# Starting the folded weight sums of the second layer earlier, in a four-batch attention and two-layer kernel

## The chip, the cores and the metric

The kernel runs on one core of a Trainium2 chip. The metric is the device time of one execution in microseconds (us). The engines are named as in the profile: PE (matmuls) with PEld (its weight loads), DVE (vector), ACT (scalar), POOL, and SP, which here only issues transfers (DMAs). POOL issues transfers too.

## The reference, cut to what matters

For 4 batches of 576 tokens, 8 heads and 32 memory slots: a softmax of `phi` over the sequence sums k and v into 32 slots per head, and the queries attend to these slots. The result, 2304 tokens by 512, goes through two layers:

```
x1 = square(relu(x @ moe_w_in)) @ moe_w_out          # 512 -> 2048 -> 512
h  = x1 @ moe2_w_in                                  # 512 -> 2048
out = (h * tanh(softplus(h))) @ moe2_w_out           # 2048 -> 512
```

## The kernel before, in words

Every float32 operand of a matmul is split into a high part (`float32r`) and a rest, and three products are summed.

**First layer.** `a_tile(b, half, f0, f1, ...)` takes 288 tokens (half of batch b) through the slices `fc` of 128 hidden units: six matmuls give `h`, ACT makes `s` from it (relu at L586, square at L587), then `g` and its rest are made (on DVE for the last batch, L593 and L594), and twelve matmuls (L540 to L542) add to four accumulators `a`, three slices later. For batches 0 and 1 the 16 slices are cut in groups of 4, 6 and 6, so there are 12 tiles, numbered `i` from 0 to 11 in the loop over `subs`. Then come the tiles (2,0), (2,1), (3,0) and (3,1), each with all 16 slices. One slice is called a step here.

**Second layer.** It is done with seven products in place of eight for each pair of 256-wide blocks (Strassen's scheme in Winograd's form). Its left operands are sums of blocks of x1 (`y_work`), its right operands sums of blocks of the weights. The weight sums are made ahead by the class `Fold`: of two raw units (512 KB each) it makes one pair, that is seven parts of 256 KB, and stores them in DRAM (`wf_i2`, `wf_o2`). There are 32 raw units (`raw_i2_0` to `15`, `raw_o2_0` to `15`; the profile leaves the 2 away), so 16 pairs. A part is cast by ACT into a stage buffer `st` (L299), DVE subtracts for the rest (L300), and POOL issues the store (L301). `Fold.tick` is called once a step: it starts a unit when it may (ACT L264), and takes one or two of the pending part steps of a pair. A stage buffer is free again when its store has landed.

**Where units are folded.** The first `EARLY` units use three raw buffers of the pool Y, which also holds the attention tiles. After tile (2,1) the loop `while fold.busy()` writes down the rest of those; the scheduler of the framework, which orders each engine's instructions by its own estimate of time, lets them run into tile (3,0). Then Y is closed and the remaining units use a pool CV in its place, ticked from tiles (3,0) and (3,1) (`tick3`).

**The seam.** After tile (3,1), `now` counts the units of the second layer: `h_step` multiplies one part `u` (loaded by `feed` from DRAM, eight ahead, L909) with a left operand, six matmuls `hb` of 384 columns (L964 to L966). ACT copies the first of a block's products out of PSUM into `ht` (L979). The parts `u57`, `u59`, ... of `wf_o2` have a second set of eight buffers, and their loads may be issued as soon as the parts are stored.

SP, ACT, DVE and POOL each work through their instructions in the order written for them, so a waiting instruction holds back all behind it on its engine.

The k and v of batch 2, first half (`kv20`, 1 MB), are loaded by `load_kv` into the one buffer with the tag "kv"; PE needs it for the sums `pk` of batch 2, in tile `i` = 10.

Of the kernel before, what the change touches and what calls it, by code (L numbers as in the profile page):

```python
# [8 lines left out]
F32R = mybir.dt.float32r  # L9
# [9 lines left out]
P = 128  # L19
# [8 lines left out]
LAG = 3  # L28
# [2 lines left out]
TT = 768  # L31
HT = TT // 2
ROLE = [0, 1, 2, 3, 0, 2, 3]
EARLY = 22


def body(tc, q, kvm, kvt, phi, w_in1, w_out1, w_in2, w_out2, out):
    nc = tc.nc

    def open_pool(name, side):  # L40
        cm = tc.tile_pool(name=name, bufs=1, side=side, reuse_waits="tile")
        return cm, cm.__enter__()
# [14 lines left out]
    cm_y, Y = open_pool("y", "right")  # L57
# [9 lines left out]
    at = (0, TAIL)  # L67
# [8 lines left out]
    def load_phi(b, p):  # L76
        nc.sync.dma_start(phi_t[p][:, at[p]:at[p] + S], phi[b, p])

    def load_kv(b, p):

        t = Y.tile([P, 2, 4, NC, D], F32, tag="kv", name=f"kv{b}{p}", bufs=1)
        nc.sync.dma_start(
            t.rearrange("p s g c d -> p s (g c d)"), kvm[b, p].rearrange("s p x -> p s x"))
        kv_t[b, p] = t

    def load_tail(b):
        t = Y.tile([P, 2, 4, D], F32, tag="kt", name=f"kt{b}", bufs=1)
        nc.sync.dma_start(
            t.rearrange("p s g d -> p s (g d)"), kvt[b].rearrange("s p x -> p s x"))
        kt_t[b] = t  # L90
# [47 lines left out]
    @contextlib.contextmanager  # L138
    def behind(table, key):

        if key is None:
            yield
        else:
            with tc.issue_after(table[key].ins):
                yield

    class Conv:
# [20 lines left out]
        def tick(self, start=True, between=None):  # L168


            ends = [x for x in self.flight if x[2] == 2]
            bits = [x for x in self.flight if x[2] == 1]
            for x in ends:
                key, u = x[0], x[1]
                if (key, u // 2) not in wt:
                    wt[key, u // 2] = tuple(
                        wo.tile([P, 2, DM], F32R, tag=f"wo{part}{u // 2}", name=f"{key}{part}{u // 2}")
                        for part in "hl")
                x[4] = [w[:, u % 2, :] for w in wt[key, u // 2]]
                nc.scalar.copy(x[4][0], x[3])  # L180
            if start and self.started < min(self.loaded, self.limit) and self.ready(*self.order[self.started]):
                key, u = self.order[self.started]
                high = self.raw[key, u][:, :, 1].bitcast(F32)
                with behind(marks, "step" if self.paced else None):
                    nc.scalar.activation(high, high, AF.Prelu, scale=2.0 ** -112, alpha=-2.0 ** 32)
                self.started += 1
                self.flight.append([key, u, 0, None, None])
            with behind(marks, self.after):
                self.fields(bits, ends, between)
            for x in self.flight:  # L190
                x[2] += 1
            for x in list(self.flight):
                if x[2] == 3 or (x[2] == 2 and x[0] == "i1"):
                    self.done.add((x[0], x[1]))
                    self.flight.remove(x)
# [38 lines left out]
    class Fold:  # L234
# [23 lines left out]
        def tick(self, start=True):  # L258
            todo, self.bits = self.bits, []
            if start and self.started < self.loaded and len(self.steps) < 5:  # L260
                key, u = self.order[self.started]
                high = self.raw[key, u][:, :, 1].bitcast(F32)
                with behind(marks, "step"):
                    nc.scalar.activation(high, high, AF.Prelu, scale=2.0 ** -112, alpha=-2.0 ** 32)  # L264
                self.started += 1
                self.bits.append((key, u))
            for key, u in todo:
                self.fields(key, u)
            for _ in range(2):
                if self.steps:  # L270
                    self.steps.pop(0)()

# [144 lines left out]
    def kv_unit(b, tag, nxt):  # L417
        for p in range(2):
            if b > 1:
                kv_soft(b, p)  # L420
                yield
            kv_turn(b, p)
            yield
            kv_mem(b, p, (0, 1), tag)
            nxt(p)
            yield
        kv_heads(b, (0, 1), tag)
        yield
# [97 lines left out]
    def drain(*lanes):  # L526
        while any(lanes):
            for lane in lanes:
                run_step(lane)
# [126 lines left out]
    def lazy(f):  # L656
        yield from f()

    def soft_both(b):
        kv_soft(b, 0)  # L660
        kv_soft(b, 1)
        yield

    def kv_later(b):
        def nxt(p):
            if p == 0 and b > 1:
                load_kv(b, 1)
            if b + 1 < B:
                load_phi(b + 1, p)
                if p == 1:  # L670
                    load_kv(b + 1, 0)
                    load_tail(b + 1)
        u = lazy(lambda: kv_unit(b, "b0", nxt))

        return [[u, 3], [iter(range(2)), 2], [u, 4]] if b > 1 else [[u, 5]]
# [17 lines left out]
    fold = Fold([(key, u) for key in ("i2", "o2") for u in range(NF)])  # L693
    fold.cap = EARLY

    def stage_0(n):
        if n % 2 == 0:
            return X.tile([P, 2, 256], F32R, tag="ys0", name=f"st{n}", bufs=2)
        return Y.tile([P, 2, 256], F32R, tag=("x", "at")[n // 2 % 2], name=f"st{n}", bufs=1)
# [4 lines left out]
    def stage_y(n):  # L704
        return Y.tile([P, 2, 256], F32R, tag=f"ys{2 + n // 2 % 2}", name=f"st{n}", bufs=2)

    fold.pool, fold.stage = Y, stage_0

    def load_page(j):

# [4 lines left out]
    for i, (f0, f1, b, half) in enumerate(subs):  # L715
        final = i == len(subs) - 1
        if i == 0:
            u = lazy(lambda: attn_unit(0, 1, lambda: load_q(1, 1)))
            lanes = [[u, 1], [soft_both(1), 1], [u, 3]] + kv_later(1) + attn_later(1, 0)
            n_steps = 3  # L720
        elif i == 1:
            assert (0, 1) in a_t
            c1.limit, c1.after, c1.paced = 2 * GROUPS[0] + 3, (0, 1), True
            n_steps = 1
        elif i == 2:
            drain(lanes)
            c1.limit, c1.after = len(c1.order), (1, 0)
            lanes, n_steps = [[iter(range(1)), 1]] + attn_later(1, 1), 1
        elif i == 3:
            drain(lanes)  # L730
            c1.after = (1, 1)
        elif i == 4:
            c1.after = None
        elif i == len(subs) - 2:
            lanes, n_steps = kv_later(2), 2
        elif final:
            drain(lanes)
            lanes, n_steps = attn_later(2, 0), 1
            load_page(0)
            load_page(1)  # L740

        def tick(fc):
            if len(c1.done) < 2 * NF:
                c1.tick()
            else:
                if not fold.loaded:
                    fold.load(3)
                if i == 10 and fc == f0 + LAG + 1:
                    fold.stage = stage_x
                if i > 9 or i == 9 and fc > f0:  # L750
                    fold.tick(start=fc % 2 == 0)

        def mid(fc):
            run_step(lanes, n_steps)

        def post(fc):
            if fc % 2 == half == 0 and fc + 2 < f1 and i != 2:
                c1.need("i1", fc + 3)
                w_part(b, fc // 2 + 1, 0, 256)
            if i == 1 and fc + 1 == f1:  # L760
                w_part(1, fc // 2, 0, 256)
            if i % 4 == 0:
                if fc >= f0 + 2:
                    c1.need("o1", fc - 2)
                if fc + 1 == f1:
                    c1.need("o1", fc)
            if half == 1 and fc + 2 == f1 and not final:

                if b == 0:
                    w_part(1, f0 // 2, 0, 256)  # L770
                else:
                    c1.need("i1", f1 + 1)
                    w_part(0, f1 // 2, 0, 256)
            if final and fc < f1 - 1:
                w_part(2, fc - f0, 0, 256)
                if fc < f1 - 2:
                    load_page(fc - f0 + 2)

        if i == 0:
            w_part(0, 0, P, 2 * P)  # L780

        a_tile(b, half, f0, f1, tick, mid, post, ("mm",) if i in (0, 1, 6) else ("mm", "b0"))
    drain(lanes)


    def tick2(fc):
        if fc == LAG + 1:
            fold.stage = stage_y
        fold.tick(start=fc % 2 == 0)

    b, nb = 2, 3
    lanes = [attn_later(b, 1), [[iter(range(2)), 2]] + kv_later(nb)]
# [283 lines left out]
    for now, (kind, i, one, two) in enumerate(plan):  # L1076
# [10 lines left out]
        if now + AHEAD < len(plan) and plan[now + AHEAD][0] == "b":  # L1087
            _, _, j, k = plan[now + AHEAD]
# [51 lines left out]
```

## Time and profile before

| what | value |
|---|---|
| median of 3 runs | 788.1 us (787.21 to 789.16) |
| the profiled execution, its own time | 790.56 us |
| its span, first to last instruction | 788.8 us |
| PE, PEld busy share of the span | 94%, 89% |
| DVE, ACT, POOL busy share | 67%, 54%, 17% |
| mean granted TensorE clock | 0.974 of full speed |

The shares are averages over stages that differ; a stage is read by its own stretch of time. Tiles 0 to 11 run to about 225 us, (2,0) and (2,1) to about 320 us, (3,0) and (3,1) to 412 us, and the second layer from there. Matmuls overlap, so the time of one is best read from start to start.

### The profile page before, as it was taken

To read this page: it belongs to the slowest core of one execution; us is meant where nothing else is said; L and a number is where in the kernel's file an instruction comes from. 1 tells how busy PE (TensorE), PEld (TensorE's weight loads), DVE (VectorE), ACT (ScalarE), POOL (GpSimd) and SP (SyncE) were. 2 spreads that over 40 slices of the span, in tenths; PEclk is the share of its full clock that TensorE was granted. 3 is DMA by queue.
4 is the path that set the end of the run, shared out by engine and by line. 5 is a ranking of instruction groups with operands and counts; after the bars stand their busy time and mean duration, and the time that the engine had idled before them with its cause. 6 is when DMAs were issued, how large, how long until landed. Compare 5 with 4: busy or idle time off the path is not lost.

```text
span 788.8 us, 16341 instructions
## 1 busy us (share of the span) xinstructions
PE 739.4 (94%) x5984; PEld 700.1 (89%) x5984; DVE 526.0 (67%) x1072; ACT 427.3 (54%) x960; POOL 136.3 (17%) x176
## 2 busy tenths in 40 slices
PE   5699999999899999989996799999999999999997
PEld 4488898998778888889995799899999999999997
DVE  3979846455757678768884559774558784556683
ACT  3577856565656677756654236452436552434552
POOL 0000000011111112232232414240112140111040
PEclk8699999999999999999998999999999999999999
DMA  9992535039888676786779978789788889788881
GB/s 333 406 406 72 187 100 195 28 124 299 279 294 297 214 246 220 258 341 208 290 254 343 295 247 292 240 268 301 240 262 251 247 265 303 244 258 251 247 265 62
DMA packets 89440, 195.85 MB, mean 248 GB/s; under 512 B 9872, under 2 KB 22672, under 8 KB 89360
## 3 DMA queue, kind: packets, MB, share of 16 engines
q1 hardware_dynamic: 80400, 165.45, 64.1%
q0 software_dynamic: 8960, 29.37, 9.6%
q8 instruction: 47, 0.77, 0.4%
q14 instruction: 33, 0.27, 0.1%
HBM read 151.78 MB, written 42.99 MB: 247 GB/s over the span
## 4 chain that ended last, share of the span: by engine, by line
PE 57%; issue 24%; POOL 7%; DMA 5%; DVE 3%; ACT 3%; SPq 1%; POOLq 0%; DVEq 0%; ACTq 0%
PE hb L964 7%; PE hb L965 7%; PE hb L966 7%; POOL wf_o L301 3%; POOL wf_i L301 3%; PE a L540 3%; PE a L541 3%; PE a L542 3%; DMA raw_i<-in_moe_w_in_dram 2%; PE h L578 1%; PE h L580 1%; PE h L579 1%; PE pw L478 1%; DMA wf_o<-st 1%; DMA u<-wf_i 1%
## 5 line engine op out<-in xcount | busy, mean ns | idle before, releaser
L540 PE MATMUL a<-g,o1h 128*128 128x288 f32 x512 | 150.5, 302 | 2.5 <-DVE ys L555 1.9
L541 PE MATMUL a<-g,o1l 128*128 128x288 f32 x512 | 149.0, 299 | 0.0
L542 PE MATMUL a<-g,o1h 128*128 128x288 f32 x512 | 132.5, 298 | 4.8 <-DVE g L594 4.8
L1009 DVE TENSOR_TENSOR opl<-a,oph 128x384 fp32r<-128x384 f32 x144 | 101.2, 723 | 50.8 <-ACT oph L1008 50.5
L964 PE MATMUL hb<-ych,u 128*128 128x384 f32 x336 | 114.8, 342 | 11.8 <-ACT ht L979 7.5
L965 PE MATMUL hb<-ycl,u 128*128 128x384 f32 x336 | 114.3, 340 | 0.0
L966 PE MATMUL hb<-ych,u 128*128 128x384 f32 x336 | 111.2, 340 | 0.0
L1008 ACT CAST oph<-a 128x384 fp32r<-128x384 f32 x144 | 73.5, 513 | 66.0 <-PE b20b L1030 5.9
L540 PEld LDWEIGHTS a<-g,o1h 128*128 128x128 f32 x512 | 97.2, 190 | 8.7 <-ACT s L586 2.9
L542 PEld LDWEIGHTS a<-g,o1h 128*128 128x128 f32 x512 | 90.3, 190 | 8.6 <-DVE g L594 6.3
L541 PEld LDWEIGHTS a<-g,o1l 128*128 128x128 f32 x512 | 97.5, 191 | 0.4 <-issue 0.4
L970 ACT ACTIVATE a<-hs 128x384 f32<-128x384 f32 x72 | 37.6, 525 | 92.2 <-DVE hs L974 92.2
L578 PE MATMUL h<-ah,wp 128*128 128x288 f32 x256 | 80.6, 316 | 5.8 <-ACT wp L484 2.8
L586 ACT ACTIVATE s<-h 128x288 f32<-128x288 f32 x128 | 52.2, 410 | 56.3 <-PE h L580 52.1
L301 POOL DMA_DIRECT2D wf_i<-st x56 | 30.3, 543 | 285.5 <-DVE st L300 278.6
L580 PE MATMUL h<-ah,wp 128*128 128x288 f32 x256 | 76.4, 299 | 0.7 <-DVE wp L485 0.7
L579 PE MATMUL h<-al,wp 128*128 128x288 f32 x256 | 76.7, 300 | 0.3 <-DVE al L468 0.3
L964 PEld LDWEIGHTS hb<-ych,u 128*128 128x128 f32 x336 | 64.3, 191 | 13.0 <-ACT ht L979 7.9
L594 DVE TENSOR_TENSOR g<-s,g 128x288 fp32r<-128x288 f32 x128 | 57.3, 450 | 26.4 <-ACT g L591 25.3
L974 DVE TENSOR_TENSOR hs<-hu,hb 128x384 f32<-128x384 f32 x72 | 39.5, 552 | 46.2 <-PE hb L966 45.8
L578 PEld LDWEIGHTS h<-ah,wp 128*128 128x128 f32 x256 | 48.7, 191 | 18.4 <-ACT s L586 5.3
L965 PEld LDWEIGHTS hb<-ycl,u 128*128 128x128 f32 x336 | 64.1, 191 | 0.0
(255 smaller groups left out, 1747.8 us busy)
## 6 DMA issues: line engine op xcount, KB each, us to landing
u<-wf_i SPq DMA_DIRECT2D x168, 256.0 KB, 3.7
u<-wf_o SPq DMA_DIRECT2D x168, 256.0 KB, 3.2
raw_i<-in_moe_w_in_dram SPq DMA_DIRECT2D x32, 512.0 KB, 5.1
raw_o<-in_moe_w_out_dram SPq DMA_DIRECT2D x32, 512.0 KB, 5.7
wf_i<-st POOLq DMA_DIRECT2D x56, 256.0 KB, 4.8
wf_o<-st POOLq DMA_DIRECT2D x56, 256.0 KB, 5.3
win1r<-w_i SPq DMA_DIRECT2D x17, 512.0 KB, 5.6
kv<-in_kvm_dram SPq DMA_DIRECT2D x5, 1024.0 KB, 9.0
```

The costliest lines, as they stand in the source:

```text
L301: nc.gpsimd.dma_start(wf[key][k, :, j], st.bitcast(F32).rearrange("p s o -> p (s o)"))
L540: nc.tensor.matmul(o, wh[:, c, cs], sh, start=first, stop=False)
L541: nc.tensor.matmul(o, wl[:, c, cs], sh, start=False, stop=False)
L542: nc.tensor.matmul(o, wh[:, c, cs], sl, start=False, stop=last)
L578: nc.tensor.matmul(ph, w[:, 0, hg, fs], hi[:, hg], start=(hg == 0), stop=False)
L579: nc.tensor.matmul(ph, w[:, 0, hg, fs], lo[:, hg], start=False, stop=False)
L580: nc.tensor.matmul(ph, w[:, 1, hg, fs], hi[:, hg], start=False, stop=(hg == 1))
L964: nc.tensor.matmul(ps, wh, yh[:, d], start=(j < 4 and d == 0), stop=False, **kw)
L965: nc.tensor.matmul(ps, wh, yl[:, d], start=False, stop=False, **kw)
L966: nc.tensor.matmul(ps, wl, yh[:, d], start=False, stop=end, **kw)
L1008: nc.scalar.copy(hi, x)
L1009: sub(lo, x, hi.bitcast(F32))
```

## The change

- `EARLY` goes from 22 to 26: four more units are folded in Y, four fewer in CV (six for ten).
- `Fold.tick` takes two part steps only while more than four are pending, otherwise one.
- The condition that let the fold tick only from the second step of `i` = 9 is gone: it ticks as soon as the first layer's weights are all converted.
- The first pair's parts use the "kv" buffer as four stage slots (`parts`), so `kv20` is no longer loaded at the end of batch 1's work but at the start of `i` = 9; new stage functions give the next parts other free tiles.
- In tiles (2,0) and (2,1) a unit may start at every third step, before at every second.

```diff
-EARLY = 22
+EARLY = 26
...
-            for _ in range(2):
+            for _ in range(2 if len(self.steps) > 4 else 1):
                 if self.steps:
                     self.steps.pop(0)()
...
                 if p == 1:
-                    load_kv(b + 1, 0)
+                    if b > 1:
+                        load_kv(b + 1, 0)
                     load_tail(b + 1)
...
+    def stage_k(n):
+        if not parts:
+            parts.append(Y.tile([P, 4, 2, 256], F32R, tag="kv", name="parts", bufs=1))
+        return parts[0][:, n % 4]
+
+    def stage_a(n):
+        return Y.tile([P, 2, 256], F32R, tag=("x", "at", "et")[n % 3], name=f"st{n}", bufs=1)
...
-    fold.pool, fold.stage = Y, stage_0
+    fold.pool, fold.stage = Y, stage_k
...
-                if i == 10 and fc == f0 + LAG + 1:
-                    fold.stage = stage_x
-                if i > 9 or i == 9 and fc > f0:
-                    fold.tick(start=fc % 2 == 0)
+                if i == 9 and fc == f0:
+                    fold.stage = stage_a
+                    load_kv(2, 0)
+                elif i in (9, 10) and fc == f0 + LAG + 1:
+                    fold.stage = stage_0 if i == 9 else stage_x
+                fold.tick(start=fc % 2 == 0)
...
     def tick2(fc):
         if fc == LAG + 1:
             fold.stage = stage_y
-        fold.tick(start=fc % 2 == 0)
+        fold.tick(start=fc % 3 == 0)
```

**At the seam, on ACT.** Before, from the last part of tile (3,1)'s accumulators on (`ys` is the copy of an accumulator, `ht` the first copy of the second layer):

```order
L299 CAST st_5335<-raw_o_15_5060 128x256
L557 COPY ys_5541<-a_4938 128x288
L299 CAST st_5193<-raw_o_13_4855 128x256
L557 COPY ys_5551<-a_4940 128x288
L299 CAST st_5227<-ct_o_12_5057 128x256
L299 CAST st_5373<-raw_o_15_5060 128x256
L299 CAST st_5331<-ct_o_14_5262 128x256
L299 CAST st_5461<-ct_o_14_5262 128x256
L299 CAST st_5368<-raw_o_15_5060 128x256
L299 CAST st_5424<-raw_o_15_5060 128x256
L299 CAST st_5428<-ct_o_14_5262 128x256
L979 COPY ht_5572<-hb_5565 128x384
```

Now, from the last cast of a part (all of the 16 pairs done) to the same copy:

```order
L299 CAST st_5126<-ct_o_14_4926 128x256
L586 ACTIVATE s_12_5386<-h_12_5377 128x288
L587 ACTIVATE s_12_5386<-s_12_5386 128x288
L586 ACTIVATE s_13_5432<-h_13_5423 128x288
L586 ACTIVATE s_14_5461<-h_14_5452 128x288
L587 ACTIVATE s_13_5432<-s_13_5432 128x288
L586 ACTIVATE s_15_5490<-h_15_5481 128x288
L587 ACTIVATE s_14_5461<-s_14_5461 128x288
L587 ACTIVATE s_15_5490<-s_15_5490 128x288
L557 COPY ys_5535<-a_5014 128x288
L557 COPY ys_5545<-a_5016 128x288
L992 COPY ht_5566<-hb_5559 128x384
```

Eight casts of parts stood behind the first `ys` copy; now the last one stands before step 12 of tile (3,1).

**At the seam, on SP.** Before, the loads of parts `u` (the number behind u is the unit of the second layer that uses it):

```order
L909 DMA u14_5641<-wf_i2_102 128x512
L909 DMA u15_5654<-wf_i2_102 128x512
L909 DMA u57_6152<-wf_o2_103 128x512
L909 DMA u59_6177<-wf_o2_103 128x512
L909 DMA u61_6205<-wf_o2_103 128x512
L909 DMA u63_6237<-wf_o2_103 128x512
L909 DMA u65_6241<-wf_o2_103 128x512
L909 DMA u67_6245<-wf_o2_103 128x512
L909 DMA u16_5665<-wf_i2_102 128x512
L909 DMA u69_6249<-wf_o2_103 128x512
L909 DMA u71_6253<-wf_o2_103 128x512
```

Now:

```order
L922 DMA u10_5590<-wf_i2_102 128x512
L922 DMA u57_6146<-wf_o2_103 128x512
L922 DMA u11_5601<-wf_i2_102 128x512
L922 DMA u59_6171<-wf_o2_103 128x512
L922 DMA u12_5613<-wf_i2_102 128x512
L922 DMA u61_6199<-wf_o2_103 128x512
L922 DMA u13_5623<-wf_i2_102 128x512
L922 DMA u63_6231<-wf_o2_103 128x512
L922 DMA u14_5635<-wf_i2_102 128x512
L922 DMA u65_6235<-wf_o2_103 128x512
L922 DMA u67_6239<-wf_o2_103 128x512
L922 DMA u15_5648<-wf_i2_102 128x512
```

The eight loads of `wf_o2` stood nearly in one block behind `u15`; now they alternate with those of `wf_i2` from `u10` on.

**Where the fold starts, on SP.** Before, `kv20` (second row) among the first layer's weight loads:

```order
L77 DMA phi0_79<-in_phi_dram 128x576
L82 DMA kv20_560<-in_kvm_dram 128x2x1024
L77 DMA phi1_81<-in_phi_dram 128x576
L164 DMA raw_o1_7_673<-in_moe_w_out_dram 128x1024
L88 DMA kt2_562<-in_kvt_dram 128x2x256
```

Now, among the first raw units of the fold:

```order
L251 DMA raw_i2_3_1889<-in_moe2_w_in_dram 128x1024
L251 DMA raw_i2_4_2103<-in_moe2_w_in_dram 128x1024
L82 DMA kv20_2139<-in_kvm_dram 128x2x1024
L251 DMA raw_i2_5_2108<-in_moe2_w_in_dram 128x1024
L251 DMA raw_i2_6_2319<-in_moe2_w_in_dram 128x1024
```

`kv20` has moved behind the load of the fifth raw unit, some 30 places down the queue. On ACT the fold's first instruction (L264 on `raw_i2_0`) moved from behind the relu `s_11` of `i` = 9 to behind `s_7` of `i` = 7, ten steps sooner.

## Rows read from the trace of the kernel before

**Rows 1.** Busy time by engine in stretches of 5 us, around the seam

```profile
core 0: us, PE busy (x) PEld busy (x) DVE busy (x) ACT busy (x) POOL busy (x), PEclk, DMA share, GB/s
415.00:420.00 5.00, 1.18 (x7) 0.86 (x5) 2.12 (x5) 0.99 (x3) 1.64 (x4) 1.00 1.01 329
420.00:425.00 5.00, 1.28 (x4) 1.28 (x5) 2.10 (x5) 2.52 (x5) 1.62 (x3) 0.58 1.04 399
425.00:430.00 5.00, 5.00 (x24) 5.00 (x23) 2.24 (x6) 2.66 (x6) 0.00 (x0) 0.74 1.04 401
430.00:435.00 5.00, 4.12 (x24) 3.80 (x22) 4.03 (x8) 2.35 (x5) 0.00 (x0) 1.00 0.75 231
435.00:440.00 5.00, 2.32 (x12) 2.03 (x12) 1.33 (x4) 0.83 (x2) 2.34 (x2) 1.00 1.01 358
440.00:445.00 5.00, 4.61 (x18) 4.64 (x19) 4.08 (x4) 1.69 (x4) 5.00 (x4) 0.66 1.00 347
445.00:450.00 5.00, 5.00 (x30) 5.00 (x29) 3.21 (x7) 0.95 (x2) 1.95 (x2) 1.00 0.71 211
```

**Rows 2.** Whom PE waited for, 411 to 450 us: sum, times, longest

```profile
PE hb L964 <- ACT ht L979: 7.5, 1, 7.5
PE hb L964 <- DMA u<-wf_i: 3.9, 2, 2.1
```

**Rows 3.** ACT in order of time: start, duration, what, idle time before

```profile
394.61 0.41 ACT L586 ACTIVATE s<-h 128x288 f32<-128x288 f32 x1
...
422.88 0.40 ACT L299 CAST st<-ct_o 128x256 fp32r<-128x256 f32 x1 [2.00 <-DMA wf_o<-st]
423.19 0.86 ACT L979 COPY ht<-hb 128x384 f32<-128x384 f32 x2
```

**Rows 4.** PE in order of time: first and last starts of two slow stretches

```profile
424.21 0.52 PE L965 MATMUL hb<-ycl,u 128*128 128x384 f32 x1
...
427.69 0.34 PE L964 MATMUL hb<-ych,u 128*128 128x384 f32 x1
...
441.37 0.52 PE L966 MATMUL hb<-ych,u 128*128 128x384 f32 x1
...
444.57 0.40 PE L964 MATMUL hb<-ych,u 128*128 128x384 f32 x1
```

**Rows 5.** SP's issues in order of time, 413 to 434 us

```profile
416.97 7.66 SPq L909 DMA_DIRECT2D u<-wf_o  x6
...
426.45 4.56 SPq L909 DMA_DIRECT2D u<-wf_o  x2
...
433.60 36.30 SPq L909 DMA_DIRECT2D u<-wf_i  x34
```

**Rows 6.** Stretches of 5 us where the fold would start, and in tile (3,0)

```profile
160.00:165.00 5.00, 5.00 (x40) 5.00 (x39) 0.92 (x2) 2.58 (x6) 0.00 (x0) 1.00 0.00 0
...
340.00:345.00 5.00, 2.63 (x20) 2.40 (x19) 2.07 (x6) 2.68 (x9) 1.08 (x2) 1.00 1.00 376
```

**Rows 7.** Whom PE waited for, 165 to 200 us, then 200 to 245 us

```profile
PE a L540 <- DVE ys L555: 0.4, 1, 0.4
...
PE a L542 <- DVE g L594: 1.9, 1, 1.9
PE a L540 <- DVE ys L555: 1.5, 1, 1.5
```

**Rows 8.** ACT at `s_12` of `i` = 8 and its first fold; PE's first batch-2 `pk`

```profile
152.34 0.41 ACT L586 ACTIVATE s<-h 128x288 f32<-128x288 f32 x1 [1.03 <-PE h L580]
...
165.31 0.66 ACT L264 ACTIVATE raw_i<-raw_i 128x512 f32<-128x512 f32 x1
...
183.14 1.08 PE L396 MATMUL pk<-kv,et 128*32 128x128 f32 x32
```

**Rows 9.** Transfers by kind: count, KB each, median us from issue to landing

```profile
wf_o<-st POOLq DMA_DIRECT2D x56, 256.0 KB, 5.3
kv<-in_kvm_dram SPq DMA_DIRECT2D x5, 1024.0 KB, 9.0
```

More of the change, by code (lines that the diff above doesn't have):

```diff
@@ L694, in body @@
     fold.cap = EARLY
+    parts = []
+    def stage_k(n):
[4 more added lines that the diff above has]
+        return Y.tile([P, 2, 256], F32R, tag=("x", "at", "et")[n % 3], name=f"st{n}", bufs=1)
     def stage_0(n):
```

## The prediction, written before the result was known

> **What bounds the kernel now.** I read the stretches of 5 us first, to find where PE is not busy, then PE's waits there, then ACT and SP in order of time, to see what those waits hang on. PE is the engine that everything else feeds, and in most stretches it is full. The large hole is the seam between tile (3,1) and the second layer. From 415 to 445 us the windows show 1.18, 1.28, 5.00, 4.12, 2.32 and 4.61 us of PE in 5, with the clock at 0.58, 0.74 and 0.66 in three of them; the window behind them holds 30 matmuls at full clock [rows 1]. PE's waits in it are one of 7.5 us for ACT's copy `ht` and two, 3.9 us together, for loads of `u` [rows 2].
>
> The first wait is a queue, not work. The copy `ht` has its input before PE falls idle, but it stands on ACT behind the casts of the last parts. The last of these waits 2.00 us for a store of `wf_o` to land and starts at 422.88; `ht` follows at 423.19 [rows 3]. So the end of the fold releases PE. The second pair of waits has the same root. SP takes 7.66 us for six loads of `wf_o` parts and 4.56 us for two more, because those parts are only just being stored; the loads of `wf_i` parts, which PE needs at once, stand behind them and flow freely only from 433.60 [rows 5]. After each hole PE runs at half clock (1.2 GHz) for a while: from 424.21 to 427.69 eleven matmuls take 3.48 us, from 441.37 to 444.57 ten take 3.20 us [rows 4], against 5.00 / 30 = 0.167 us each at full clock (2.4 GHz) [rows 1].
>
> So the seam loses 7.5 + 3.9 us in waits, (3.48 - 11 x 0.167) = 1.6 us and (3.20 - 10 x 0.167) = 1.5 us by the clock: 14.5 us of the 30.
>
> **The change, part by part.**
>
> *The fold ends sooner.* Two pairs (four units) are taken out of the stretch after Y is closed. In the new order the last cast of a part stands on ACT before step 12 of tile (3,1). That step's relu started at 394.61 [rows 3], and ACT has no other late input there, so the last cast comes near 394 us instead of 422.88, and its store, 5.3 us at the median [rows 9], has landed near 400 us. The tile ends near 410. Nothing of the fold is then left at the seam: `ht` waits for its own matmuls alone. That takes away the 7.5 us and, with the hole, the 1.6 us at half clock: **-9.1 us**.
>
> *The loads at the seam.* The waits for `u` need not vanish. From 415 to 445 us the DMAs moved (329 + 399 + 401 + 231 + 358 + 347) GB/s x 5 us = 10.3 MB [rows 1]. Eight stores of the fold's tail (256 KB each, the eight casts behind the first `ys` copy) leave the stretch: 2.1 MB. The other 8.2 MB stay: the `wf_i` parts, the eight `wf_o` parts, four loads of `y1` for the next tile (1.6 MB by their shape). At the highest sustained rate of the rows, 401 GB/s, they take 20.5 us, while PE's work in the stretch is 30 - 14.5 = 15.5 us. If all of them had to land before PE could go on, the seam would shrink by 9.5 us and no more; if the 1.6 MB for the next tile came out of the way, by 13.5; if no wait for `u` were left, by 14.5. Below, there is no reason that the waits grow as long as the DMAs keep 401 GB/s, so 9.1. I take 10.5, near the bound by bytes, since SP's one queue holds wanted and unwanted loads in turn: a further **-1.4 us** (bounds 0 and -5.4).
>
> The Trainium skill's page "DMA: Bandwidth & Descriptors", section Specifications, gives a core's limit at the HBM as about 358 GB/s. By it the 8.2 MB would need an estimated 22.9 us, and the seam would shrink by only 7.1 us. The trace disagrees in part: two windows in a row show 399 and 401 GB/s, though the windows in which PE also works show 358 and 347 [rows 1].
>
> *The fold starts ten steps sooner.* What leaves the seam is now done from `s_7` of `i` = 7 on, some 26 us sooner: five steps lie between 152.34 and the fold's first instruction at 165.31, so a step is 2.6 us there [rows 8]. That stretch has room: in 160 to 165 us DVE is busy 0.92, ACT 2.58 of 5 us, the DMAs not at all [rows 6]. The nearest stretches with the fold in them show its price: from 165 to 200 us the longest PE wait on DVE is 0.4 us, so 0.3 us in 26; from 200 to 245 us two waits make 3.4 us, or 2.0 us in 26, but there the attention of batch 2 shares DVE [rows 7]. A gain is excluded, as PE is full there today. I take the nearer row, rounded up: **+0.5 us** (bounds 0.3 and 2.0).
>
> *k and v of batch 2 later.* They hide behind first-layer matmuls. Their buffer is taken by the first pair's parts; the last of these is cast before `s_12` of `i` = 8, at 152.34. Its store needs some 5.3 us, the load then 9.0 [rows 9]: landed near 167 us, and PE wants them at 183.14 [rows 8]. The margin is 16 us: **0**. On SP, `kv20` now waits for those stores with raw units and the y1 stores behind it; they lose a few us that nothing waits for, since the raw unit next behind it is folded only in the last step of `i` = 9, some 15 us later.
>
> *The wider spread, the stage slots.* One part step for two and starts at every third step lower DVE's and ACT's density in tiles (2,0) and (2,1), but the new units fill it again: the new order still starts a pair every six steps, as the old did. **0**. In tile (3,0) the three last pairs of Y run out at the same steps as before, one step sooner, beside the same prefetch of `u`. The stall at 340 to 345 us (PE 2.63 of 5) [rows 6] I leave: **0**, with -2.4 if it goes and +2.4 if it doubles.
>
> *Tile (3,1).* DVE loses the folding of four units there; PE loses filler, for three units of `hb` (18 matmuls, 3.0 us) that stood inside the tile now stand behind it. If DVE is late with `g` nothing covers it: bounds 0 and +3.0; I take 0, since DVE has less to do.
>
> **The sum**: -9.1 - 1.4 + 0.5 = -10.0 us. It is made against the profiled execution's own 790.56 us, which gives 780.6. That execution lay 2.5 us above the median of 788.1, so the median should come to 778.1.
>
> **The rivals.**
>
> *The whole seam clears.* The waits for `u` hang on SP's blocked queue [rows 5], and the new order has the blocked loads' stores landed 10 us before. For it: the 231 GB/s window, in which the DMAs were not even full [rows 1]. Against it: the bytes above. -14.5 + 0.5: 774.
>
> *The loads become the bound.* Where PE and loads ran together the rows show 347 and 358 GB/s [rows 1]; at 350 the 8.2 MB take 23.4 us, and the seam shrinks by 6.6 only: -6.6 + 0.5 gives 782. This is what the Trainium skill's limit would do by itself.
>
> *The fold does not end sooner.* The new order is only an order. The six units of CV wait for their raw loads, and those for Y's close; if they come late, the casts, and with them all of ACT, slip towards the seam and `ht` waits as before: 788. Against it: ten units needed until 422.88, and six are four fewer.
>
> *Slower: `kv20` late.* One mechanism: the slots that hold the first parts are freed late, `kv20` lands after 183.14 and PE's `pk`, with everything behind it, waits. Each us past 183 costs one. To end 0.3% (2.4 us) slower than before it must eat the 10 us too and land near 196, 29 us later than I work out. Nothing in the rows speaks for so much.
>
> **How the numbers follow.** My forecast (seam shrinks by 9 to 12 us, 776 to 780) gets 0.50, the cleared seam 0.22, loads as the bound 0.16, no sooner end 0.08, slower 0.04. The predicted time is that of the first. The range: below, the cleared seam with the stall at 340 us gone as well (774 - 2.4, so 771); above, loads as the bound with the early fold at its upper price and 2.4 us more in tile (3,0) (782 + 1.5 + 2.4, so 786). Within 0.3%, about what a measurement of this kernel can tell from no change, is 785.7 to 790.5. The first two cases and most of the third are faster: 0.86; the fourth is the same, with a rest of the third: 0.09; slower 0.05.
>
> **What would show it right or wrong.** Right: no wait of PE for `ht` at the seam, the last cast of a part (L299) some 12 us or more before the last `ys` copy, the clock at 1.00 in the window behind tile (3,1), waits for `u` of 1 to 5 us; parts cast from about 140 us with no PE wait above half a us until 165; `pk` of batch 2 at its old time or sooner. Wrong: casts of parts among the last steps of tile (3,1), or waits for `u` that take the place of the one for `ht`, or a PE wait for `kv`.

## The result, and the profile after

The median went from 787.65 us (787.17 to 789.16, four executions in this measurement) to 779.86 us (777.2 to 782.17, four): a ratio of 0.9897, 95% interval 0.9857 to 0.9936. The profiled execution took 781.31 us by its own time, with a span of 779.5 us and a mean granted clock of 0.976. Against the execution profiled before (790.56 us) that is -9.25 us; the sum had said -10.0. The median was put at 778.1 and came 1.8 us above that.

Whom PE waited for from 395 to 450 us, in the changed kernel (sum, times, longest):

```profile
PE hb L977 <- DMA u<-wf_i: 1.6, 2, 1.1
```

The wait for `ht` of 7.5 us [rows 2] is gone; of the waits for `u` 1.6 us are left. The stretches of 5 us from 405 us on (columns as in [rows 1]):

```profile
405.00:410.00 5.00, 5.00 (x39) 5.00 (x38) 0.92 (x2) 0.80 (x2) 0.00 (x0) 1.00 0.00 0
410.00:415.00 5.00, 5.00 (x30) 5.00 (x29) 1.91 (x4) 1.82 (x3) 0.00 (x0) 1.00 0.97 298
415.00:420.00 5.00, 5.00 (x30) 5.00 (x30) 2.35 (x5) 2.37 (x5) 0.00 (x0) 1.00 0.99 321
420.00:425.00 5.00, 5.00 (x30) 4.74 (x28) 3.75 (x7) 3.18 (x7) 1.02 (x1) 1.00 1.05 395
425.00:430.00 5.00, 3.36 (x14) 2.96 (x14) 2.05 (x4) 0.19 (x1) 1.23 (x2) 0.82 1.06 380
430.00:435.00 5.00, 5.00 (x25) 4.85 (x25) 2.37 (x4) 2.09 (x5) 4.92 (x3) 0.84 1.05 382
```

PE is full across the end of tile (3,1) and for 15 us behind it, at full clock. From 425 to 435 us it runs 39 matmuls where 60 would fit: (60 - 39) x 0.167 = 3.5 us are lost, in place of 14.5 us. ACT in order of time shows why:

```profile
396.51 0.41 ACT L299 CAST st<-ct_o 128x256 fp32r<-128x256 f32 x1 [0.86 <-DMA wf_o<-st]
...
408.29 0.40 ACT L557 COPY ys<-a 128x288 f32<-128x288 f32 x1 [5.45 <-PE a L542]
409.08 0.40 ACT L557 COPY ys<-a 128x288 f32<-128x288 f32 x1 [0.39 <-PE a L542]
410.52 0.48 ACT L992 COPY ht<-hb 128x384 f32<-128x384 f32 x1 [1.04 <-PE hb L979]
```

The last cast of a part stands 12.6 us ahead of the last `ys` copy, and `ht` waits for PE, not PE for `ht`. It comes at 410.52, where it came at 423.19 [rows 3].

Tile (3,0) did not gain but lost. From 325 to 355 us PE is busy 25.01 us of 30, before 26.65. The hole of [rows 6] stands some 2 us sooner and is a little deeper (a wait of 2.7 us, before 2.4):

```profile
340.00:345.00 5.00, 2.25 (x10) 2.03 (x9) 2.87 (x9) 3.25 (x10) 1.24 (x3) 0.79 1.03 405
345.00:350.00 5.00, 5.00 (x36) 5.00 (x35) 2.87 (x10) 2.17 (x6) 1.70 (x4) 0.87 0.69 270
```

ACT and DVE around it in order of time, and whom PE waited for from 335 to 350 us:

```profile
338.12 0.43 ACT L299 CAST st<-raw_o 128x256 fp32r<-128x256 f32 x1 [3.76 <-DMA wf_o<-st]
341.69 0.41 ACT L299 CAST st<-ct_o 128x256 fp32r<-128x256 f32 x1 [3.14 <-DMA wf_o<-st]
...
347.89 0.42 ACT L299 CAST st<-raw_o 128x256 fp32r<-128x256 f32 x1 [2.54 <-DMA wf_o<-st]
...
342.13 0.43 DVE L300 TENSOR_TENSOR st<-ct_o,st 128x256 fp32r<-128x256 f32 x1 [3.12 <-ACT st L299]
...
PE a L542 <- DVE g L594: 2.7, 1, 2.7
```

The casts of the last parts made in Y wait for a stage slot, that is for a store to land while the DMAs move 405 GB/s. The casts hold the relus behind them on ACT, the subtractions behind the casts (L300) hold DVE, and PE waits 2.7 us for `g`. A wait for ACT that was not there before stands ahead of it:

```profile
327.47 0.40 PE L578 MATMUL h<-ah,wp 128*128 128x288 f32 x1 [1.88 <-ACT s L586]
```

### The profile page after: what moved, and what is told of

It reads as the page before. It is cut to its first block, busy times and chain, and to the rows that moved or that the text cites. A ratio compares the mean times of both kernels' runs of the same rounds, so it can differ in the third digit from the quotient of the medians.

```text
span 779.5 us, 16347 instructions
## 1 busy us (share of the span) xinstructions
PE 738.7 (95%) x5984; PEld 700.4 (90%) x5984; DVE 526.1 (67%) x1072; ACT 426.5 (55%) x960; POOL 134.3 (17%) x176
## 4 chain that ended last, share of the span: by engine, by line
PE 63%; issue 19%; DMA 5%; POOL 5%; DVE 3%; ACT 3%; SPq 0%; POOLq 0%; DVEq 0%; ACTq 0%
PE hb L977 7%; PE hb L978 7%; PE hb L979 7%; PE a L540 4%; PE a L542 4%; PE a L541 4%; POOL wf_i L301 3%; DMA raw_i<-in_moe_w_in_dram 2%; PE h L578 2%; PE h L580 2%; PE h L579 2%; DMA u<-wf_i 2%; POOL wf_o L301 2%; DMA wf_o<-st 1%; PE pw L478 1%
## 5 line engine op out<-in xcount | busy, mean ns | idle before, releaser
L540 PE MATMUL a<-g,o1h 128*128 128x288 f32 x512 | 149.7, 302 | 4.3 <-ACT g L591 3.4
L1022 DVE TENSOR_TENSOR opl<-a,oph 128x384 fp32r<-128x384 f32 x144 | 102.8, 733 | 51.1 <-ACT oph L1021 50.8
L542 PE MATMUL a<-g,o1h 128*128 128x288 f32 x512 | 130.2, 298 | 4.9 <-DVE g L594 4.9
L977 PEld LDWEIGHTS hb<-ych,u 128*128 128x128 f32 x336 | 63.5, 189 | 2.5 <-DMA u<-wf_i 2.4
L979 PEld LDWEIGHTS hb<-ych,u 128*128 128x128 f32 x336 | 63.4, 189 | 0.0
```

The lines of the kernel that those rows point to most:

```text
L540: nc.tensor.matmul(o, wh[:, c, cs], sh, start=first, stop=False)
L542: nc.tensor.matmul(o, wh[:, c, cs], sl, start=False, stop=last)
L977: nc.tensor.matmul(ps, wh, yh[:, d], start=(j < 4 and d == 0), stop=False, **kw)
L979: nc.tensor.matmul(ps, wl, yh[:, d], start=False, stop=end, **kw)
L1022: sub(lo, x, hi.bitcast(F32))
```

## The experiments

Two of the change's parts might have cleared the seam: the cap of 26 (two pairs fewer behind Y's close) and the earlier start. My theory ahead of the runs was that the cap does it and that the start is a small price. The rivals are the start itself, the bytes at the seam, and the wider spread. All ratios are to the kernel before, run beside each group on the same chip; its medians there were 793.42, 789.19 and 792.67 us. A profile shows one execution: that of b26 is the slowest of its twelve, those of hold and spread2 are the fastest of their six.

### The cap and the start, one without the other

**Run cap22**: everything of the change but the cap.

```diff
-EARLY = 26
+EARLY = 22
```

> The changed kernel with the fold's cap back at 22: everything else of the change stays (start at s_7 of i = 7, the place of k and v for the first parts, the spread of one step for two, kv20 later), but ten units, not six, are left for the stretch after Y is closed. My theory (the seam's gain is the ACT queue: ht stood behind the last casts, and four units fewer end it sooner): the last cast of a part comes back to the seam near 420 us, PE waits 6 to 8 us for ht again, the seam loses 13 to 15 us instead of 3.5, and the time is 788 to 791 us. Rival A (the earlier start is what pays, by a lighter DVE and ACT in tiles (2,0) to (3,1), and the seam's wait is a by-product): the casts end well ahead of the last ys copy with ten units too, and the time stays at 778 to 782. Rival B (half of it: 24 units would have been enough, so the wait comes back only by some 2 or 3 us): 782 to 785.

Measured: 0.9796 (0.9744 to 0.9848), median 775.97 us. No wait for `ht`; the last cast comes at 398.02. My theory as written fell: ten units are left for CV, as before the change, and `ht` is free all the same (rival A), with a time below the 778 to 782 us of that rival too. Tile (3,0) has no hole either:

```profile
335.00:340.00 5.00, 5.00 (x40) 5.00 (x39) 4.79 (x14) 4.08 (x11) 1.35 (x3) 1.00 1.05 395
340.00:345.00 5.00, 5.00 (x40) 5.00 (x39) 4.56 (x14) 3.45 (x9) 1.34 (x3) 1.00 1.03 401
345.00:350.00 5.00, 5.00 (x40) 5.00 (x40) 4.67 (x15) 3.68 (x10) 1.83 (x4) 1.00 0.92 293
```

Part of this comes back later. Near the end of the fold, in tile (3,1), PE now waits for `g`, which it does not do in the changed kernel:

```profile
394.01 0.80 PE L542 MATMUL a<-g,o1h 128*128 128x288 f32 x4 [2.08 <-DVE g L594]
```

**Run b26**: the kernel before with the cap alone.

```diff
-EARLY = 22
+EARLY = 26
```

> The kernel before with the cap at 26 alone: the fold starts where it did (i = 9, second step), with the old spread and the old kv20. My theory: at the seam it is like the changed kernel (no wait for ht, seam 10 us shorter), but the four units that are not started sooner must be folded in front of Y's close: the drain in tile (3,0) works through two pairs more than before, PE's stall at 340 to 345 us grows by 4 to 10 us (a pair takes some 14 us at the pace of the steps, part of it covered), and most of the seam's gain is given back: 782 to 788 us. Rival (the early start is not needed, since DVE and ACT have room in tiles (2,0) to (3,0) and the drain takes it up): 777 to 780, no larger stall than the changed kernel's.

Measured: 0.9936 (0.9902 to 0.9971), 787.50 us. Most of the gain is given back, as expected, but in another place: no deep hole in tile (3,0), where PE's longest wait is 1.2 us, while the seam's waits are back (PE from 411 to 450 us, then ACT in order of time):

```profile
PE hb L964 <- DMA u<-wf_i: 2.7, 2, 1.8
PE hb L964 <- ACT ht L979: 2.5, 1, 2.5
PE hb L964 <- ACT ys L557: 1.8, 1, 1.8
```

```profile
417.28 0.42 ACT L299 CAST st<-raw_o 128x256 fp32r<-128x256 f32 x1 [1.86 <-DMA wf_o<-st]
417.94 0.40 ACT L557 COPY ys<-a 128x288 f32<-128x288 f32 x1 [0.24 <-DMA wf_o<-st]
...
424.47 0.40 ACT L299 CAST st<-ct_o 128x256 fp32r<-128x256 f32 x1 [3.16 <-DMA wf_o<-st]
424.78 0.86 ACT L979 COPY ht<-hb 128x384 f32<-128x384 f32 x2
```

With only six units left for CV the last cast is as late as before the change (424.47; 422.88 in [rows 3]). So the cap alone does not end the fold sooner. Why, the start of the CV stretch tells: ACT's first instruction on a unit of it stands at 384.98 here, 358.19 in the kernel before. In b26, the kernel before, the changed kernel and cap22:

```profile
384.98 0.68 ACT L264 ACTIVATE raw_o<-raw_o 128x512 f32<-128x512 f32 x1 [2.35 <-DMA raw_o<-in_moe_w_out_dram]
...
358.19 0.67 ACT L264 ACTIVATE raw_o<-raw_o 128x512 f32<-128x512 f32 x1
...
356.98 0.67 ACT L264 ACTIVATE raw_o<-raw_o 128x512 f32<-128x512 f32 x1
...
333.37 0.69 ACT L264 ACTIVATE raw_o<-raw_o 128x512 f32<-128x512 f32 x1 [3.23 <-DMA raw_o<-in_moe_w_out_dram]
```

**Runs early_only and half22** take this further. early_only is cap22 with the old spread too, so that the start (with k and v's place) is alone; half22 is cap22 with a start half way.

```diff
 early_only, against cap22
-            for _ in range(2 if len(self.steps) > 4 else 1):
+            for _ in range(2):
...
-        fold.tick(start=fc % 3 == 0)
+        fold.tick(start=fc % 2 == 0)
 half22, against cap22
                     fold.load(3)
+                if i == 7 or i == 8 and fc < f0 + 2:
+                    return
```

> The changed kernel with cap 22 and with the old spread, so that of the change only the earlier start (with k and v's place and the later kv20 that it needs) is left. My theory after the first runs (the start alone moves the fold's end, and the cap is what makes the stall in tile (3,0)): no wait for ht above 1 us, no stall at 340 to 345, the last cast within 2 us of the run with cap 22 and the new spread, and 0.976 to 0.983 of the kernel before, 4 to 8 us under the changed kernel. Rival (the spread is what let the earlier start pay): the ratio is 0.985 or more, with new waits of PE for g or s in tiles (2,0) and (2,1).

> Cap 22, the new spread, and a start in the middle: the raw units are loaded as early as in the changed kernel, but the first one is started from the third step of i = 8, five steps before the old start and five behind the new. My theory (the fold's end follows its start, and ht waits as soon as the last cast falls behind the last ys copy): the last cast comes 5 to 14 us later than with the full early start (398 us there), some 403 to 412, PE waits 0 to 4 us for ht, and the time is 0 to 5 us above that of the full early start, 0.980 to 0.988 of the kernel before. Rival (the end is set elsewhere, by the raw loads behind Y's close or by the order near the end, so that a few steps at the start don't matter): the last cast stays within 2 us of 398 or goes back to 420 at once.

Measured: early_only 0.9812 (0.9769 to 0.9855), half22 0.9868 (0.9827 to 0.9908). In early_only the last cast comes at 396.74 and tile (3,0) has no hole. half22 shows the dose; its last cast is 3.1 us ahead of the first `ys` copy, and `ht` is just not held up:

```profile
408.17 0.41 ACT L299 CAST st<-ct_o 128x256 fp32r<-128x256 f32 x1 [0.25 <-DMA wf_o<-st]
411.30 0.40 ACT L557 COPY ys<-a 128x288 f32<-128x288 f32 x1 [2.72 <-PE a L542]
412.10 0.40 ACT L557 COPY ys<-a 128x288 f32<-128x288 f32 x1 [0.40 <-PE a L542]
412.39 0.49 ACT L994 COPY ht<-hb 128x384 f32<-128x384 f32 x1
```

Still half22 stands 4.6 us above early_only in the same group (779.85 against 775.29), with no wait for `ht` in either, so the start is worth more than that wait. Some 2.4 us of it lie in tile (3,0): from 325 to 355 us PE is busy 27.64 us of 30 in half22 and all 30 in early_only. Where the rest lies is not shown.

Read from the profiles in this way, the CV stretch gives one rule:

| kernel | units in CV | its first unit starts | last cast | us per unit | PE waits for `ht` and `ys` |
|---|---|---|---|---|---|
| before | 10 | 358.19 | 422.88 | 6.5 | 7.9 |
| b26 | 6 | 384.98 | 424.47 | 6.6 | 4.3 |
| half22 | 10 | 346.68 | 408.17 | 6.1 | none |
| after | 6 | 356.98 | 396.51 | 6.6 | none |
| cap24 (below) | 8 | 344.48 | 396.44 | 6.5 | none |
| early_only | 10 | 333.34 | 396.74 | 6.3 | none |
| cap22 | 10 | 333.37 | 398.02 | 6.5 | none |

A unit takes 6.1 to 6.6 us there, however many there are. Two pairs moved ahead of Y's close put off the start of the CV stretch by as much as they shorten it: 26.8 us later for four units in b26, 23.6 us between cap22 and after. What ends the fold sooner is the start alone. The fold's first instruction (`raw_i` of its first unit on ACT), in the changed kernel, half22, cap22 and b26:

```profile
139.04 0.67 ACT L264 ACTIVATE raw_i<-raw_i 128x512 f32<-128x512 f32 x1
...
150.47 0.66 ACT L264 ACTIVATE raw_i<-raw_i 128x512 f32<-128x512 f32 x1
...
140.35 0.68 ACT L264 ACTIVATE raw_i<-raw_i 128x512 f32<-128x512 f32 x1
...
167.13 0.66 ACT L264 ACTIVATE raw_i<-raw_i 128x512 f32<-128x512 f32 x1
```

From there to the last cast it is 257.5, 257.7, 257.7 and 257.3 us, and 257.6 us in the kernel before (from 165.31 [rows 8]). half22 and cap22 differ in the start alone: 10.1 us later at the start, 10.2 us later at the end.

### What the cap of 26 does

**Run cap24**: one pair fewer than the change, one more than before.

```diff
-EARLY = 26
+EARLY = 24
```

> The changed kernel with cap 24, one pair more than the kernel before has in front of Y's close. My theory by now (the earlier start moves the fold's end; every pair of cap beyond what the start makes room for is folded in the drain at the first steps of tile (3,0) and holds back Y's close): between cap 22 and cap 26, 0.980 to 0.987, a stall of PE in 330 to 350 us of about half the changed kernel's, the last cast within 3 us of both. Rival (the cap costs nothing by itself, and the stall at 340 us comes and goes with the order of the rest): the same ratio as cap 22, or as cap 26, with no order between the three.

**Run cap22_2** is cap22 once more, beside it; **after2** is the changed kernel once more, beside early_only and half22. Neither has an edit against its twin.

> The changed kernel with cap 22 once more, as the yardstick on this chip: of the three beside it, two differ from it in one thing each (cap 24; the spread loads at the seam), and the third has cap 26. Expected 0.977 to 0.983 of the kernel before, as in its first run.

> The changed kernel once more, as the yardstick on this chip for the three beside it; nothing is altered. Both theories: 0.985 to 0.990 of the kernel before, no wait of PE for ht, the stall at 340 to 345 us in its place.

Measured: cap24 0.9769 (0.9733 to 0.9806), cap22_2 0.9792 (0.9759 to 0.9826), after2 0.9861 (0.9813 to 0.9909). So cap 24 is as good as 22, below the range I gave it: the order by pairs that I expected does not hold. Cap 26 looks dearer with the wider spread (0.9897 and 0.9861 against 0.9796 and 0.9792). With the old spread it does not: spread2 (below) and early_only differ in the cap alone, and stand at 0.9814 and 0.9812, though in different groups. In tile (3,0) PE's longest wait from 325 to 352 us is none in cap22, cap22_2 and early_only, 1.2 us in cap24, and 2.7 and 3.5 us in after and after2. ACT's waits for stores of `wf_o` in that stretch sum to 3.3, 2.5 and 0.6 us without a hole, and to 10.7 and 9.8 us in after and after2; but also to 9.4 us in cap24, where PE loses little. So the waits go with the hole and are not enough for it. The full early start with cap 22 has its own wait instead: one of 2.0 to 2.5 us for `g`, between 388 and 396 us, in all five kernels that have both.

### The wider spread

**Run spread2**: the changed kernel with the old spread (the edit of early_only, cap 26 kept).

> The changed kernel with the old spread: two part steps at each tick, starts at every second step in tiles (2,0) and (2,1). My theory (the wider spread is worth 0): within 2 us of the changed kernel, 778 to 782 us, with the steps of tiles (2,0) to (2,1) at most 2 us later and the last casts of parts no later at the seam. Rival A (the thinner stream is what brings tile (2,0) in 2 to 4 us sooner than before): those steps come 3 to 4 us later and the time is 782 to 785. Rival B (the wider spread puts pairs off until Y's close and makes the larger stall in tile (3,0)): the stall shrinks, 774 to 777.

Measured: 0.9814 (0.9765 to 0.9863), 777.30 us, with a hole of 2.0 us in tile (3,0). With cap 26 the old spread looks 0.5 to 0.8% better than after (0.9897) and after2 (0.9861), but the intervals touch and the runs are of different groups. With cap 22 it makes no difference: 0.9812 against 0.9796 and 0.9792, and 0.9743 against 0.9742 below. The profiles speak for a cost with cap 26: from 325 to 355 us PE is busy 28.04 us in spread2, and 25.01 to 26.39 us in the four profiles with cap 26 and the wider spread. That is one profile against four, so the cost is not shown; that the wider spread gains is not to be seen.

### The loads at the seam

**Run hold** puts 12 loads off: eight of `wf_o` parts that PE needs 47 units later, and four of `y1` for the next tile.

```diff
+            with behind(held, n - 24 if n >= 56 and n % 2 else None):
+                held[n] = nc.sync.dma_start(t.bitcast(F32).rearrange("p s o -> p (s o)"), wf[key][k, :, j])
...
+            with behind(held, 44 if i == 1 else None):
                 nc.sync.dma_start(r[k, n], y1[:, 2 * k:2 * k + 2, c0:c0 + HT])
```

> The changed kernel with 12 loads of the seam held back on SP's queue: the eight early loads of wf_o parts (odd u from u57) stand behind the load of the u 24 numbers before, and the four loads of y1 for the next tile behind u44. Nothing is left out. My theory (what is left at the seam, two or three waits for u of 4.7 us together, is bytes that PE does not yet need, in front of those that it needs): 8 x 256 KB + 1.6 MB leave the stretch from 410 to 430 us, the waits for u fall below 1.5 us, the clock stays at 1.00 in 425 to 435, and the time is 2.5 to 4 us below the changed kernel's, 776 to 777.5. Rival A (the loads are bound by latency or by the ring of eight u, so that taking others away does not help): waits of 3 to 5 us stay, 779 to 781. Rival B (the held loads come late for the second product): PE waits for u or y1 near 465 us, and the time is 780 or more.

Measured: 0.9855 (0.9804 to 0.9905), 781.69 us: nothing gained that these runs can tell. The waits for `u` are gone from 395 to 445 us and come back at 455 to 460 us, where the held loads now meet those of `wf_i` (whom PE waited for from 445 to 540 us; three stretches):

```profile
PE hb L979 <- DMA u<-wf_i: 1.6, 2, 1.4
```

```profile
425.00:430.00 5.00, 5.00 (x31) 5.00 (x30) 2.99 (x7) 1.29 (x3) 0.00 (x0) 1.00 0.74 190
...
450.00:455.00 5.00, 5.00 (x30) 4.79 (x28) 3.31 (x7) 1.74 (x4) 0.23 (x1) 1.00 1.06 388
455.00:460.00 5.00, 3.39 (x14) 2.95 (x14) 4.22 (x4) 1.96 (x4) 4.92 (x3) 0.86 1.05 384
```

**Runs hold2, hold2_26 and hold2_s2** spread the same loads evenly, with cap 22, cap 26, and cap 22 with the old spread. The text put down for hold2 calls it the changed kernel; what ran had cap 22, so its twin is cap22 or early_only, and hold2_26 is the run that the text describes.

```diff
+            with behind(held, (10 + (n - 57) // 2 * 5 if n < 72 else n - 24) if n >= 56 and n % 2 else None):
...
+            with behind(held, {(0, 0): 22, (0, 1): 32, (1, 1): 42, (1, 0): 50}[k, n] if i == 1 else None):
```

> The changed kernel with the same 12 loads as in the run that held them, spread now instead of put off: one wf_o part behind every fifth wf_i part from u10 on, one load of y1 for the next tile behind each of u22, u32, u42 and u50. Nothing is left out. My theory (the whole stretch from 405 to 465 us is near what the DMAs carry, 380 to 400 GB/s at their best, so what counts is that the extra 3.7 MB lie evenly beside the 256 GB/s that PE eats): about 330 GB/s throughout, no wait for u above 0.5 us at either end, and 3 to 5 us less than the changed kernel beside it. Rival (held or not, the sum of bytes is paid somewhere): waits for u of 1.5 us or more with half clock behind them come back at some point of 405 to 465 us, and the gain is under 1.5 us.

> The spread loads at the seam (one wf_o part behind every fifth wf_i part, four loads of y1 behind u22, u32, u42, u50) with the cap at 26, which is what the text of the run hold2 describes; the kernel that ran there had cap 22. My theory (the seam's waits for u and the stall in tile (3,0) are two things and add up): no wait for u above 0.5 us from 395 to 470 us, the stall at 330 to 350 us as in the changed kernel, 0.979 to 0.985, some 4 us above hold2 and 3 to 5 us below the changed kernel. Rival (with the fold out of the way the two meet, and the seam gives back what the stall took): the same as hold2, 0.972 to 0.977.

> Cap 22, the spread loads at the seam, and the old spread of the fold's steps (two part steps at each tick, starts at every second step): of the change only the earlier start is left, with the seam's loads put in order. My theory (the wider spread is worth nothing, its sign unknown): within 2 us of hold2, 0.971 to 0.978, which would be the fastest of all with it. Rival (with cap 26 the old spread looked 3 to 5 us better; if that was real, it shows here too): 0.968 to 0.971.

Measured: hold2 0.9742 (0.9702 to 0.9783), 770.08 us, beside early_only's 775.29; hold2_s2 0.9743 (0.9712 to 0.9773), 771.34 us, beside cap22_2's 776.84; hold2_26 0.9816 (0.9781 to 0.9851), 777.89 us. The bytes were most of the seam's last loss: in hold2 the only wait for `u` from 395 to 530 us is one of 0.4 us, and the stretches are even:

```profile
PE hb L979 <- DMA u<-wf_i: 0.4, 1, 0.4
```

```profile
420.00:425.00 5.00, 5.00 (x31) 5.00 (x30) 3.80 (x7) 2.70 (x6) 1.38 (x1) 1.00 1.02 367
425.00:430.00 5.00, 5.00 (x31) 5.00 (x30) 3.16 (x6) 2.46 (x5) 1.02 (x1) 1.00 0.93 307
430.00:435.00 5.00, 5.00 (x31) 5.00 (x30) 3.00 (x5) 1.05 (x2) 1.55 (x1) 1.00 0.96 328
435.00:440.00 5.00, 4.61 (x27) 4.29 (x26) 2.76 (x5) 1.93 (x5) 1.31 (x2) 1.00 0.94 325
```

Spread, the loads give about 5 us at cap 22 by the medians of one group (5.2 and 5.5 us; each pair differs in the spread of the fold's steps too, which made no difference at cap 22). The profiles place less of it at the seam and behind: from the start of the last `ys` copy to the end it is 364.2 and 365.3 us in hold2 and hold2_s2, and 366.9 to 367.2 in early_only, cap22 and cap22_2, so 1.6 to 3.0 us. Where the rest comes from is open. hold2_26 has the hole of tile (3,0), a wait of 3.0 us, and stands 0.7% above hold2, as it should if the two losses add up. hold2 and hold2_s2 are the fastest kernels of the study, with the changed kernel's earlier start, its cap undone, and the seam's loads in order.

## Why the prediction was right, and where not

**The sum and its two halves.** Cut at the relu of step 8 of tile (3,1), which starts at 384.13 us before and at 385.30 after, the way there grew by 1.2 us (0.5 was put down), and the rest shrank from 404.7 to 394.2 us, 10.5 us, which is what the seam was given. That so small a difference as 0.7 us in the first half is real can't be said: it is 380.0 in early_only and 383.8 in cap22_2, which differ in the spread alone.

**The fold ends sooner, -9.1.** Right in size and in mechanism: the wait for `ht` and its half clock are gone, and the last cast is at 396.51, where 394 was put down. Wrong in the cause. The step counted "two pairs taken out of the stretch after Y is closed" and took it that this stretch starts when it did. It does (356.98 for 358.19), but only because the start of the whole fold lies ten steps sooner; without that (b26) it starts 27 us later and a gain of 0.6% is left, and with the start alone (cap22) ten units end at the same time as six. The number held because it was read from the new order of the whole change, the start included.

**The fold ten steps sooner, +0.5, "a gain is excluded".** This is the step that failed, and its failing did not show in the sum. I priced the start by the stretch in which the units are now folded, and excluded a gain since PE is full there. The gain lies later. At the seam it is the -9.1 that I booked for the cap. In tile (3,0) PE is busy all 30 us from 325 to 355 in the five kernels with the full early start and cap 22, before 26.65; the wait for `g` in tile (3,1) takes some 2 us of it back. With cap 26 and the wider spread the gain in tile (3,0) is gone (25.01 us in the changed kernel). That the start's gain there and the cap's price left the first half only 1.2 us longer is luck. In the stretch itself the price was as put down: no wait of PE from 135 to 165 us.

**The stall in tile (3,0), 0.** Too low. Over the six windows from 325 to 355 us, 5 us less PE's busy time at the window's granted clock comes to 7.6 us, before 5.0: an estimated 2.6 us more are lost, where +2.4 was the price of a stall that doubles. Nor is the stall simply left over. With the early start it is gone at cap 22 and there at cap 26; with the late start it is there at cap 22 [rows 6], and at cap 26 (b26) PE's longest wait is 1.2 us. So it hangs on start and cap together.

**Tile (3,1), 0.** Right for the change: PE waits for nothing from 352 us to the tile's end. The late `g` that the text feared is what the kernels with cap 22 show, with 2.0 to 2.5 us.

**The loads at the seam, -1.4.** The seam's loss fell by 11.0 us, 9.1 of them with `ht`, so 1.9 for the loads. The bound by bytes, from which the value was taken, pointed the right way: the DMAs run at 395, 380 and 382 GB/s where PE waits, and putting bytes off (hold) only moves the wait. But the seam shrank by more than my bound of 9.5, which took all 8.2 MB as due in those 30 us; spread to where there is room (hold2) they cost next to nothing. The rival "loads become the bound", which rested on 350 GB/s beside PE and a seam shorter by 6.6 us, did not come: the three windows are above that rate. The Trainium skill's page "HBM Reference", section Specifications (TRN2), says that a core streaming alone measures well above the share of 358 GB/s, at about 425 GB/s. The three windows, at 380 to 395 GB/s, lie between the two figures.

**k and v of batch 2, 0.** Right. SP issues `kv20` at 156.59, a load of `kv` lands 5.8 us after its issue at the median from 155 to 185 us, and PE's sums start at 184.14, 1.0 us later than before [rows 8], with no wait for `kv`. By that median the load had landed near 162, so the margin is some 22 us, not 16. A later load was not tried.

**The rivals.** The whole seam cleared only with the loads spread as well; a time of 774 (cap24, 774.15) came without that, by what tile (3,0) gave back. The slower case had no sign in any run. That the fold would end no sooner is what the cap gives by itself (b26).

What stays open is how the hole in tile (3,0) comes from start, cap and spread: in cap24 and in the changed kernel ACT waits for stores for much the same time, and PE loses much more in the second.

## What to carry to other kernels

Work that streams through the whole kernel in a fixed order ends when it started plus its length; moving a border between two of its stretches only changes where it stalls. So price an earlier start at its end, not where it starts. And where transfers and PE both run near their limits, look at which bytes are not yet needed: spread out they cost next to nothing here, put off in a block they cost the same later.

## What the runs showed of the hardware

A short wait of PE did not always bring the half clock (1.2 GHz). In the changed kernel waits of 0.56 and 1.07 us, which end at 425.65 and 428.04, are followed by a stretch at half clock, so that the means of the two windows of 5 us are 0.82 and 0.84. In cap22 four waits of 0.32 to 0.46 us, which end from 427.58 to 432.83, leave the clock at 1.00 (the two windows of cap22 that hold them):

```profile
425.00:430.00 5.00, 4.18 (x21) 3.24 (x21) 3.16 (x6) 2.09 (x5) 2.09 (x2) 1.00 1.06 379
430.00:435.00 5.00, 4.14 (x22) 3.50 (x21) 2.73 (x4) 0.21 (x1) 4.44 (x4) 1.00 1.05 384
```

Over those 10 us the one runs 39 matmuls, the other 43. Nor was one wait like another: the wait of 2.08 us in tile (3,1) of cap22 left the next window (395 to 400 us) at a mean clock of 1.00, one of 2.07 us in the same place of cap22_2, the same kernel, was followed by 0.66. Executions of one kernel differed more than ahead of the study, 772.5 to 779.8 us in cap22, and the kernel before had medians of 787.65 to 793.42 us on four occasions, so differences of half a per cent between groups were not built on.
